# Soft MoE behind an attention, one core: w1's rows dealt to the partitions by chunks of 128, and the slot sums reading x in packed columns

## The chip, the core and the metric

The kernel runs on one core of one Trainium2 chip. The metric is the device time of one execution in microseconds (us); lower is better. TensorE (PE, with its weight loads as PEld), VectorE (DVE), ScalarE (ACT) and GpSimd (POOL) work side by side, each through its own queue in order; transfers between DRAM and SBUF run on 16 DMA engines. All loads of this kernel are issued from POOL's queue and convert float32 to bf16 on the way; the stores of the output are issued from SP's.

## The reference

An attention over 8 batches, 12 heads, 448 tokens and heads of 64, with one more term in the softmax's sum, feeds a soft mixture of 8 experts with 4 slots each:

```python
def _attn_ref(q, k, v):
    scale = 1.0 / np.sqrt(q.shape[-1])
    scores = scale * np.matmul(q, k.transpose(0, 1, 3, 2))
    m = np.max(scores, axis=-1, keepdims=True)
    e = np.exp(scores - m)
    attn = e / (np.sum(e, axis=-1, keepdims=True) + np.exp(-m) + 1e-09)
    return np.matmul(attn, v)

def _moe_ref(x, phi, w1, w2):            # x (3584, 768), phi (768, 32)
    logits = x @ phi
    d = np.exp(logits - logits.max(0, keepdims=True))
    d /= d.sum(0, keepdims=True) + 1e-09
    slot_input = (d.T @ x).reshape(E, S_per_e, D)
    for e in range(E):                   # w1[e] (768, 1024), w2[e] (1024, 768)
        h = np.maximum(slot_input[e] @ w1[e], 0.0)
        slot_out[e] = h @ w2[e]
    c = np.exp(logits - logits.max(1, keepdims=True))
    c /= c.sum(1, keepdims=True) + 1e-09
    return c @ slot_out.reshape(n_slots, D)
```

Between the two, x is the attention's output with the heads side by side: a row for each token, 768 columns.

## The kernel before

**Attention.** The 96 heads are taken in 48 pairs. A loop of 49 steps, each of two half-steps (about 5 us a step), runs several pairs at once in different phases: `T` transposes q and k on PE (L205), `A` computes scores and their row maxima on DVE (L227, L231, L240), `Bk` scores once more with the maxima subtracted by a second product (L302, L305) and the exponentials on ACT (L308), `AV` the products with v (L339), `N1` and `N2` the division on POOL (L351, L367 to L376; on DVE for the last four pairs), which write x, and `PX` x's transposes, one pair two steps later (L399, copied by ACT in L405). Six pairs are one batch of 448 tokens: x of a batch lies in `x[:, i, :]` with 128 tokens on the partitions, four blocks i, and 768 columns; two such buffers alternate.

**Slots, batch by batch.** `P(b)` returns the pieces of the mixture's first part for a batch, which the loop places in later half-steps: logits (`l_mm`, L434: x transposed, 24 blocks of 128x128 as weights, phi's 32 columns streamed), the running maximum and the exponentials `cd`, then `s_mm`, the slot sums d.T @ x. `s_mm` (L482 to L490) fills one PSUM tile `ps_s` with 7 parts of 32 slots: for each of the KC = 6 parts j of x's columns four matmuls, one for each block i of tokens, with a 128x128 piece of x as weights and 32 columns of `cd` streamed, and then four matmuls with a column of ones, for the sums of d. `s_add` adds `ps_s` to `acc` on DVE (L499, L501 for the first batch). For the batches 0 to 5 `s_mm` is placed in every sixth step, the second half (the matmuls start at 88, 119, 149, 180, 211 and 241 us), for batch 6 in the 47th step (259 us); for batch 7 it runs behind the loop (273 us), where `s_last` (L506) writes the sums to `siT`.

**Which column of x is where.** `siT[p, j, slot]` is the stationary operand of the experts' first layer (`hidden`, L673), which multiplies it with `w_sb["w1", e][p, j, :]` and sums over partitions p and parts j. So the column of x that part j of the slot sums puts on partition p has to be the row of w1 that lies on p as part j. In the kernel before both are 6p + j: `load_part` (L107, L108) reads w1 and w2 of an expert as `"(p j) f -> p j f"`, six (w1) or eight (w2) neighbouring rows to a partition, and `s_mm` takes for part j every sixth column of x. w2's rows are matched in the same way by `turn` (L680), which takes every eighth column of the hidden layer.

**Loads.** All go through POOL's queue in program order, among POOL's other work. At the end of a step come, where it is their turn: q and k some steps ahead of their use (L141, 336 KB each), v (L145, L146), and w1 in halves of three rows per partition (`load_half`, L114, L115; 768 KB as bf16): the first half of an expert in the steps 1, 4, 7, 10, 13, 16, 22 and 25, the second in the step after; w2 of three experts in the same way from step 28. The tile W has room for these 11 weights and nothing else reads or writes it before the loop ends. The other five w2 go into R, the tile that holds the attention's buffers, piece by piece as these are done with (`part_at` from step 38, and L647, L648, L662, L663). The last piece is three rows of expert 7 (L663), into the place of an x buffer that the last `s_mm` reads.

**After the loop.** `hidden` for experts 0 to 3 and 4 to 7, `turn`, `slots` (L687: the second layer, with w2 streamed; experts 4 to 7 by halves of the columns), a rearrangement of the slots' outputs (L725), and c @ slot_out in 28 tiles of 128 tokens (L743), scaled on ACT and DVE (L749, L751) and stored in seven transfers (L754).

Of the kernel before, what the change touches and what calls it, by code (L numbers as in the profile page):

```python
# [31 lines left out]
def kernel(  # L32
# [17 lines left out]
    KC = DD // 128  # L50
# [53 lines left out]

    def load_part(i, z0, z1):
        kind, e = halves[i]
        src = (moe_w1 if kind == "w1" else moe_w2)[e].rearrange("(p j) f -> p j f", p=128)  # L107
        gdma(out=w_sb[(kind, e)][:, z0:z1, :], in_=src[:, z0:z1, :])  # L108

    def load_half(i, z, t=None):  # L110

        if t is not None:
            w_view(i, t)
        n = (KC if halves[i][0] == "w1" else FK) // 2  # L114
        load_part(i, z * n, (z + 1) * n)  # L115
# [6 lines left out]
    with ExitStack() as at:  # L122
# [290 lines left out]
        def P(b):  # L413
            l, new = lb[b % 2], lb[(b + 1) % 2][:, 4, :]
            eng = nc.gpsimd if b < B - 2 else nc.vector
            x = xb[b % 2]
# [65 lines left out]
            def s_mm():  # L482
                ps = pa([128, KC + 1, NS], F32, "ps_s")
                for j in range(KC + 1):
                    for i in range(4):

                        w = x[:, i, :].rearrange("p (d j) -> p j d", j=KC)[:, j, :] if j < KC else \
                            ones[:, int(i == 3):int(i == 3) + 1].to_broadcast([128, 128])
                        nc.tensor.matmul(ps[:, j, :], w, v["cd"][:, 4 + i, :], start=(i == 0), stop=(i == 3))  # L489
                v["ps_s"] = ps  # L490
# [25 lines left out]
            if b < B - 1:  # L516
                return [both(lambda: l_mm(range(KC)), l_ev, c_max), both(l_turn, c_sub), both(s_max, d_sub),
                        both(exps, corr)] + ([c_turn, both(s_mm, s_add)] if late(b) else [both(s_mm, s_add), c_turn])
            return [lambda: l_mm(range(PB - 2)),
                    lambda: l_mm([PB - 2]),  # L520
                    both(lambda: l_mm([PB - 1]), l_ev, l_turn, lambda: keep_busy(2), s_max,
                         d_sub, lambda: exps(4, 8), corr, lambda: keep_busy(5), s_mm, s_last, lambda: keep_busy(2),
                         c_max, c_sub, lambda: exps(0, 4)),
                    c_turn]
# [50 lines left out]
        for s in range(NPAIR + 1):  # L575
# [69 lines left out]
            for i, z0, z1 in part_at.get(s, ()):  # L645
                load_part(i, z0, z1)
        load_part(14, 1, 8)  # L647
        load_part(15, 0, 1)  # L648
        nc.vector.reduce_max(fold, ident.rearrange("p (i s) -> p s i", i=4), axis=AX.X)
# [135 lines left out]
```

## Time and profile before

| | us |
|---|---|
| median of 3 runs (lowest to highest) | 321.62 (321.37 to 322.61) |
| the profiled execution, its own time | 321.49 |
| span of its profile | 319.7 |

| engine | busy us | share of the span | instructions |
|---|---|---|---|
| PE | 284.4 | 89% | 5072 |
| PE's weight loads (beside PE) | 165.9 | 52% | 5074 |
| DVE | 253.0 | 79% | 575 |
| ACT | 250.1 | 78% | 546 |
| POOL | 194.6 | 61% | 402 |
| DMA, the queue of POOL's loads | 31776 packets, 42.52 MB | 81.8% of 16 engines | 106 issues |

The mean granted clock of PE is 0.951 of full speed. In the chain of waits that ended last PE has 53% of the span, DVE 22% and ACT 11%; line 489 of the slot sums has 3%.

How to read it: the busy shares are means over a long loop and a tail that have different limits. In a timeline or chain row the first number is the start and the second the length in us, L489 is line 489 of the kernel, `ps_s<-cd,R` names the tile that is written and those that are read, and brackets give the idle time of that engine just before the row and what ended it. PEld is the load of a matmul's stationary operand; it runs beside the matmul before it. The length of one matmul holds its way through the array, so a row of matmuls that follow each other is read by the distance of their starts. A DMA row is the issue on its engine; the transfer lands later. In the table of windows the columns are: window, its length, then busy us and the number of instructions for PE, PEld, DVE, ACT and POOL, the granted clock, the share of the 16 DMA engines' time that packets took (over 1 where packets overlap) and the GB/s written.

### The profile page before, as it was taken

Reading aid. Unit: us, or ns where it says so; the run is one execution under the profiler, and the core shown is the slowest. Engines: PE = TensorE matmul, PEld = TensorE weight load, DVE = VectorE, ACT = ScalarE, POOL = GpSimd, SP = SyncE. Lnnn points to the kernel's source line nnn. Section 1 sums busy time; section 2 is a strip of 40 time slices with the busy share of each in tenths; the row PEclk is TensorE's granted clock in tenths of the full one; section 3 lists DMA queues with packets and bytes.
Section 4 is the critical chain, followed back from the end, with each engine's and each line's share of the span. In section 5 each row is a group of like instructions: output and inputs, shape, how many; then the busy total and the mean of one; then the engine's idle time right before and its main releaser. Section 6 shows DMA issues by size and latency. Waiting matters only on the chain.

```text
span 319.7 us, 12146 instructions
## 1 busy us (share of the span) xinstructions
PE 284.4 (89%) x5072; PEld 165.9 (52%) x5074; DVE 253.0 (79%) x575; ACT 250.1 (78%) x546; POOL 194.6 (61%) x402
## 2 busy tenths in 40 slices
PE   2898999999999999999999999999999997997800
PEld 1444556555566566656656665566555555561100
DVE  5888999998989989997999799989998354337910
ACT  2367699999989998999999999999998983217800
POOL 8651797868768968695978688867775723100000
PEclk9999999999999999999999999999999999897555
DMA  7990799999999999678999999997445899964998
GB/s 87 143 135 4 105 208 203 187 193 162 184 180 162 197 148 180 86 112 146 187 154 187 180 170 162 182 193 130 76 51 100 149 157 193 200 126 178 425 431 344
DMA packets 32838, 54.30 MB, mean 170 GB/s; under 512 B 2576, under 2 KB 27920, under 8 KB 32272
## 3 DMA queue, kind: packets, MB, share of 16 engines
q0 software_dynamic: 31776, 42.52, 81.8%
q1 hardware_dynamic: 1008, 11.01, 8.2%
q8 instruction: 39, 0.64, 0.7%
q14 instruction: 15, 0.12, 0.1%
HBM read 85.03 MB, written 11.01 MB: 300 GB/s over the span
## 4 chain that ended last, share of the span: by engine, by line
PE 53%; DVE 22%; ACT 11%; issue 4%; DMA 3%; POOL 2%; POOLq 0%; ACTq 0%
DVE mx L231 15%; PE ps_b L302 11%; PE ps_av L339 11%; PE ps_a L227 9%; PE ps_b L305 7%; PE ps_t L205 5%; ACT R L308 5%; DMA R<-in_moe_w_dram 3%; PE ps_s L489 3%; PE ps_o L743 3%; ACT R L208 2%; DVE mx L240 2%; DVE R L210 2%; ACT R L405 2%; ACT W L749 2%
## 5 line engine op out<-in xcount | busy, mean ns | idle before, releaser
L308 ACT ACTIVATE R<-ps_b 128x448 bf16<-128x448 f32 x336 | 158.3, 560 | 13.4 <-PE ps_b L305 9.9
L231 DVE TENSOR_REDUCE mx<-ps_a 128x1 f32<-128x448 f32 x288 | 160.7, 615 | 9.5 <-PE ps_a L227 9.0
L302 PE MATMUL ps_b<-R 64*128 64x448 bf16 (+1 forms) x384 | 82.6, 358 | 2.1 <-ACT R L405 1.8
L305 PE MATMUL ps_b<-mT,sel 64*128 64x448 bf16 (+1 forms) x384 | 78.9, 352 | 0.0
L227 PE MATMUL ps_a<-R 64*128 64x448 bf16 x288 | 68.8, 364 | 5.3 <-DVE mx L231 2.9
L367 POOL TENSOR_TENSOR R<-ubuf,rec 128x384 bf16<-128x384 f32 x44 | 36.3, 824 | 47.9 <-DVE rec L361 22.4
L339 PE MATMUL ps_av<-R 128*128 128x65 bf16 (+1 forms) x1536 | 64.8, 196 | 0.1
L339 PEld LDWEIGHTS <-R 128*128 128x128 bf16 (+1 forms) x1536 | 50.2, 100 | 23.9 <-issue 19.7
L205 PEld LDWEIGHTS <-R 64*64 64x64 bf16 x1344 | 31.1, 113 | 16.6 <-issue 6.1
L205 PE MATMUL ps_t<-ident,R 64*64 64x64 bf16 x1344 | 31.5, 197 | 5.3 <-DMA R<-in_q_dram 4.3
L302 PEld LDWEIGHTS <-R 64*128 64x128 bf16 (+1 forms) x384 | 19.4, 97 | 30.5 <-issue 25.6
L305 PEld LDWEIGHTS <-sel 64*128 64x128 bf16 (+1 forms) x384 | 21.3, 97 | 23.2 <-issue 15.9
L405 ACT CAST R<-ps_x 128x512 bf16<-128x512 f32 x47 | 27.9, 593 | 6.3 <-PE ps_x L399 6.2
L240 DVE TENSOR_REDUCE mx<-ps_a 128x1 f32<-128x448 f32 x48 | 29.6, 617 | 0.4 <-PE ps_a L237 0.3
L208 ACT COPY R<-ps_t 128x896 bf16<-128x896 bf16 x20 | 18.4, 918 | 10.8 <-PE ps_t L205 10.8
L351 ACT COPY ubuf<-ps_av 128x455 f32<-128x455 f32 x44 | 25.1, 571 | 1.2 <-PE ps_av L339 1.0
L227 PEld LDWEIGHTS <-R 64*128 64x128 bf16 x288 | 17.8, 94 | 14.5 <-issue 3.6
L376 POOL TENSOR_TENSOR R<-ubuf,rec 128x128 bf16<-128x128 f32 x44 | 17.6, 400 | 3.7
L237 PE MATMUL ps_a<-R 64*64 64x448 bf16 x96 | 18.5, 381 | 0.6 <-DVE mx L231 0.6
L399 PE MATMUL ps_x<-ident,R 128*128 128x128 bf16 x192 | 18.7, 218 | 0.0
L247 POOL TENSOR_SCALAR R<-mx 64x6 bf16<-64x6 f32 (+5 forms) x51 | 13.6, 266 | 8.1 <-DVE mx L231 4.7
L108 POOL DMA_DIRECT2D R<-in_moe_w_dram x15 | 8.4, 566 | 15.7 <-PE ps_s L489 6.7
(126 smaller groups left out, 368.5 us busy)
## 6 DMA issues: line engine op xcount, KB each, us to landing
W<-in_moe_w_dram POOLq DMA_DIRECT2D x22, 768.0 KB, 10.2
out_dram<-W SPq DMA_DIRECT2D x3, 2688.0 KB, 11.2
R<-in_v_dram POOLq DMA_DIRECT2D x32, 192.0 KB, 6.0
R<-in_q_dram POOLq DMA_DIRECT2D x15, 336.0 KB, 6.0
R<-in_k_dram POOLq DMA_DIRECT2D x15, 336.0 KB, 7.3
R<-in_moe_w_dram POOLq DMA_DIRECT2D x3, 768.0 KB, 7.7
out_dram<-W SPq DMA_DIRECT2D x3, 768.0 KB, 4.3
R<-in_moe_w_dram POOLq DMA_DIRECT2D x1, 1344.0 KB, 11.5
```

The source lines that it names most:

```text
L205: nc.tensor.transpose(ps[r, a, c:c + 64], src[r, pl, tok * D:(tok + 1) * D], ident[r, r])
L208: nc.scalar.copy(t, ps)
L227: nc.tensor.matmul(pss[hl][:, 0:S], t[r, 0, i * 128:(i + 1) * 128], t[r, 1, :], start=True, stop=True)
L231: nc.vector.reduce_max(mx[g][:, c:c + 1], pss[hl][:, 0:S], axis=AX.X)
L240: nc.vector.reduce_max(mx[g][:, c:c + 1], ps[:, 0:S], axis=AX.X)
L302: nc.tensor.matmul(outs[hl], t[rs[hl], 1, cols], t[rs[hl], 0, :], start=True, stop=False)
L305: nc.tensor.matmul(outs[hl], sel[rs[hl], 2 * pl + hl:2 * pl + hl + 1].to_broadcast([64, m]), mT[mg(n)][rs[hl], :], start=False, stop=True)
L308: nc.scalar.activation(e, p[:, 0:S], AF.Exp, scale=scale)
L339: nc.tensor.matmul(o, eT[n, i, hl][:, qc], vp[g % 2][:, 2 * pl + hl, i, 0:W65], start=(i == 0 and u == 0 and hl == 0), stop=(i == 3), skip ...
L351: (nc.scalar.copy if on_pool(n) else nc.vector.tensor_copy)(u, src)
L367: eng.tensor_mul(x[:, 0:3, c:c + 128].rearrange("p i (h d) -> p i h d", h=2), u[:, 0:6, 0:D].rearrange("p (i h) d -> p i h d", h=2), rec[: ...
L405: nc.scalar.copy(xT[:, pb, :], pss[0])
```

## The change

Two lines. w1's rows are dealt to the partitions by chunks of 128: part j on partition p is now row 128j + p. The slot sums take for part j the 128 neighbouring columns of x from 128j on, so that the same column of x meets the same row of w1. w2 is loaded as before.

```diff
     def load_part(i, z0, z1):
         kind, e = halves[i]
-        src = (moe_w1 if kind == "w1" else moe_w2)[e].rearrange("(p j) f -> p j f", p=128)
+        src = (moe_w1 if kind == "w1" else moe_w2)[e].rearrange("(j p) f -> p j f" if kind == "w1" else "(p j) f -> p j f", p=128)
         gdma(out=w_sb[(kind, e)][:, z0:z1, :], in_=src[:, z0:z1, :])
...
                 for j in range(KC + 1):
                     for i in range(4):
 
-                        w = x[:, i, :].rearrange("p (d j) -> p j d", j=KC)[:, j, :] if j < KC else \
+                        w = x[:, i, j * 128:(j + 1) * 128] if j < KC else \
                             ones[:, int(i == 3):int(i == 3) + 1].to_broadcast([128, 128])
                         nc.tensor.matmul(ps[:, j, :], w, v["cd"][:, 4 + i, :], start=(i == 0), stop=(i == 3))
```

The order of instructions is the same on every engine; on POOL the 16 loads of w1 change from 128 runs of 3072 elements to 128 x 3 runs of 1024.

## The prediction

> **What bounds the kernel now.** I read the page first: PE, DVE and ACT are each busy for 78 to 89% of the span, so no one engine explains it and the stage around the change has to be read by itself. Then the instructions of the two lines that do the same kind of product with a strided and an unstrided stationary operand (min/median/max ns):
>
> ```profile
> L489 PEld LDWEIGHTS <-R x192: 124/144/152, 88.1 to 274.7; 128*128 128x128 bf16 x192
> L489 PE MATMUL ps_s<-cd,R x192: 189/198/234, 88.2 to 274.7; 128*128 128x32 bf16 x192
> ...
> L434 PEld LDWEIGHTS <-R x192: 95/96/99, 64.8 to 270.8; 128*128 128x128 bf16 x192
> L434 PE MATMUL ps_l<-phi_sb,R x192: 176/176/190, 64.8 to 270.8; 128*128 128x32 bf16 x192
> ```
>
> Same shapes, 128x128 loaded and 128x32 streamed; the weights of L489 step 6 elements, those of L434 step 1. A duration is not a rate, so next the timeline (start us, length us, engine) around the first slot sum and around one block of L434:
>
> ```profile
> 88.13 1.20 PEld L489 LDWEIGHTS <-R 128*128 128x128 bf16 x24
> 88.16 1.27 PE L489 MATMUL ps_s<-cd,R 128*128 128x32 bf16 x24
> ...
> 89.27 0.25 PE L489 MATMUL ps_s<-cd,ones 128*128 128x32 bf16 x4
> 89.35 0.23 PEld L399 LDWEIGHTS <-R 128*128 128x128 bf16 x4
> 89.37 0.38 PE L399 MATMUL ps_x<-ident,R 128*128 128x128 bf16 x4
> 89.56 0.39 DVE L501 COPY acc<-ps_s 128x224 f32<-128x224 f32 x1 [1.33 <-PE ps_s L489]
> ...
> 89.79 0.59 ACT L405 CAST R<-ps_x 128x512 bf16<-128x512 f32 x1 [0.60 <-PE ps_x L399]
> ```
> ```profile
> 64.82 0.75 PE L434 MATMUL ps_l<-phi_sb,R 128*128 128x32 bf16 x24
> 65.51 0.32 PE L339 MATMUL ps_av<-R 128*64 128x65 bf16 x8
> ```
>
> From the first strided matmul to the first `ones` matmul, 88.16 to 89.27, 24 pairs take 1.11 us, 46.2 ns each. In L434 24 pairs take 65.51 - 64.82 = 0.69 us, 28.7 ns each. While the slot sum runs, DVE stands idle for 1.33 us behind it and ACT for 0.60 us behind the transposes queued after it (brackets): at this spot PE alone sets the pace. The same brackets stand at the sums near 119, 149, 181 and 212 us (1.40 and 0.60), and 0.94 and 0.94 near 242 us.
>
> The chain of waits (start, length) and the PE timeline then tell what sets the end:
>
> ```profile
> 275.17 11.12 DMA R<-in_moe_w_dram
> 286.30 0.04 issue
> 286.34 1.96 PE ps_so L687 x41
> ```
> ```profile
> 286.34 1.95 PE L687 MATMUL ps_so<-R,W 128*32 128x384 bf16 x41 [0.19 <-DMA R<-in_moe_w_dram]
> ```
>
> The last piece of w2 lands at 286.3 and PE waits only 0.19 us for it: two paths meet there, PE's and that of the transfers. Busy time by windows (the last two columns are the DMA share and GB/s written) and the POOL timeline say since when the transfers are backlogged:
>
> ```profile
> 256.00:260.00 4.00, 3.87 (x67) 2.28 (x62) 2.06 (x7) 4.00 (x11) 1.14 (x3) 1.00 0.82 122
> 260.00:264.00 4.00, 4.00 (x67) 2.17 (x66) 2.60 (x9) 3.12 (x8) 0.76 (x2) 1.00 1.11 202
> 276.00:280.00 4.00, 4.00 (x76) 2.05 (x69) 0.86 (x4) 1.99 (x4) 0.00 (x0) 1.00 1.03 199
> ```
> ```profile
> 255.48 1.66 POOL L108 DMA_DIRECT2D R<-in_moe_w_dram  x3 [1.00 <-PE ps_b L305]
> ```
>
> Three loads are issued at 255.48, released by PE; from about 258 on the queue is full at some 200 GB/s until 286. So a PE that is faster before 255 moves the end; what it gains after 255 meets a full queue.
>
> **The change, part by part.**
>
> *Slot sum without a stride* (L487/489). No instruction is added, removed or moved. Each of the 8 sums has 24 affected pairs. The new pitch is bounded below by the `ones` pairs of L489, whose weights step 0: 89.27 to 89.37, 4 pairs in 0.10 us, 25 ns; above by today's 46.2 ns (no gain). I take 28.7 ns from L434, which has the same shapes and a packed operand. Gain per sum: 24 x (46.2 - 28.7) = 0.42 us (0 to 0.51). It is less than the 0.60 us that ACT and the 1.33 us that DVE now wait there, so all three engines, and POOL, which waits for ACT's copy, start the next step 0.42 us earlier, and everything behind follows.
>
> Six sums (88, 119, 149, 180, 211, 241 us) lie before the issue at 255.48: 6 x 0.42 = 2.5 us. The seventh (259 us) and the eighth (273 us) advance PE by 0.84 us more, but the queue is full by then, so the last landing moves from 286.3 to about 283.8 only. PE's wait there grows from 0.19 to 0.19 + 0.84 = 1.0 us. What stands behind the landing (rest of L687, L725, output, stores) is unchanged and moves by 2.5 us.
>
> *w1 dealt by chunks* (L107). The 16 loads of half an expert's w1, issued between 36 and 165 us, have the same bytes; each partition's one run of 12 KB in DRAM (6 KB written) becomes three of 4 KB (2 KB written). w2's loads, which set the tail, keep theirs. Two costs:
>
> POOL's issue: L108 with 128 runs takes 0.57 us; L141 with 384 runs (3 per partition, the new count) 0.76 to 0.81. So +0.19 to +0.24 us, at most 3.8 us on POOL in all. It is covered by POOL's idle time: behind the issue at 103.31 comes L469, and then L367 after 0.41 us of idle; behind that at 87.41, 2.4 us of idle; the shortest I found is 0.32 us at 44 us. L367's product is transposed by PE two steps (about 10 us) later. Without this cover the cost would be its 3.8 us.
>
> The transfer: the queue is nearly full in this stage (the window 36 to 128 us has a DMA share of 1.09 and 183 GB/s, against 200 in the tail). The issues of 41 to 46 us and their times to landing:
>
> ```profile
> W<-in_moe_w_dram POOLq DMA_DIRECT2D x1, 768.0 KB, 10.7
> R<-in_q_dram POOLq DMA_DIRECT2D x1, 336.0 KB, 6.6
> R<-in_k_dram POOLq DMA_DIRECT2D x1, 336.0 KB, 7.5
> ```
>
> Issued at 41.57 (q), 42.40 (k) and 43.15 (w1), they land at 48.16, 49.86 and 53.86: k, in runs of 896 B, takes 1.70 us behind q, 202 GB/s; w1, in runs of 6 KB, 4.00 us, 197 GB/s. In a full queue short runs are as fast as long ones: 0. The other bound is from the trace's packet records (median ns by bytes written: 896 in 88, 3072 in 248, 6144 in 474): some 22 ns a packet plus 73.6 ns per KB of 1000 bytes. Three of 2048 B then take 3 x 173 = 519 for 474 ns; with 8 partitions on each of 16 DMA engines that is +0.36 us per load. I take 0 on the path, because the loads behind have slack: k issued at 102.55 lands at 109.5 and is first read at 117.8 (8.3 us); v issued at 94.92 lands at 100.6 and POOL copies it at 106.4 (5.8 us). Two loads per three steps, +0.72 us, do not use that up; w1 itself is read after 266 us.
>
> Sum: -2.5 us on 321.49, the profiled execution's own time (span 319.7 and 1.8 around it), gives 319.0. The median of the runs shown, 321.62, is 0.13 above that execution; I leave the forecast at 319.0.
>
> **Rivals.**
>
> *All eight sums count.* If the queue in the tail has some room after all (in the 4 us before 260 its share is 0.82), or the later issues also bring it forward, the end moves by 8 x 0.42 = 3.4 us, at most 8 x 0.51 = 4.1: 318.1, down to 317.4. Against it: the landings from 264.6 to 286.3 follow one another at 200 GB/s without a gap.
>
> *The stride costs nothing, no change.* If what makes L489 slow is not the step but where the tile lies or the order of its sums, the gain is 0: 321.5. Against: the transposes of L680, with a step of 8, also load in 146 to 148 ns at the median, those of L399, step 1, in 97. The Trainium skill ("SBUF — State Buffer", "Door 1: The DMA port swizzle") gives 8 elements as the step that bf16 may take for free in SBUF's lines of 16 bytes. By that figure a step of 6 is free and this would be the outcome; the trace disagrees with 144 against 96 ns. (The same place asks for two accesses to a line; 12 bytes apart they mostly don't share one, and by that condition the trace agrees.)
>
> *w1's new runs are slow in DRAM: slower.* One partition's three runs lie 512 KB apart, and no load of this trace reads so. Between two groups of three steps (about 15.6 us apart) the queue works 8.0 us on w1, 3.4 on q and k and 1.8 on v, so some 2.4 us are free. With x us more per w1 load, the backlog grows by 2x - 2.4 + 0.2 a group (0.2 being half of a sum's gain), over 6 groups, until v's 5.8 us are gone; then PE waits. It eats the 2.5 us gain at 6 (2x - 2.2) = 5.8 + 2.5, so x = 1.8, a load of 5.8 instead of 4.0 us. At x = 2.5 it would be 16.8 - 5.8 - 2.5 = 8.5 us slower: 330. Against it: even the first loads, with start-up, ran at 135 to 143 GB/s on the page's strip (5.6 us for such a load, x = 1.6).
>
> **How the numbers follow.** Forecast, six sums: 0.61. All eight: 0.18. No change: 0.10. Slow w1: 0.11. Below 0.5%, 1.6 us, a measurement of this kernel can't be told from no change. Faster takes the first two, 0.79; a little of the first could fall under 1.6 us, and a little of the third over it. Same 0.10, slower 0.11. The likeliest case alone spans 318.4 (pitch 25 ns) to 319.6. The range reaches down to all eight sums at their bound, 317.4, and up to just under no change, 321.3; it leaves out some 0.2.
>
> **What would show it.** Right: L489's weight loads near 96 ns; the 24 pairs in 0.69 us; ACT's wait before L405 in those steps about 0.18, DVE's before L499 about 0.98; sums 0.42 us earlier each time; L108's issues at 0.8 us; 4096 packets more; the last landing near 283.8, with PE waiting about 1 us for it in L687. Wrong: L489 still at 140 ns; w1 landing more than 13 us after its issue; a wait of L205 for q or k after 40 us; a last landing before 283 (all eight) or after 285.

## The result and the profile after

| | us, median (lowest to highest) | runs |
|---|---|---|
| before, beside the changed kernel | 321.69 (321.37 to 322.61) | 4 |
| changed | 318.13 (317.18 to 319.22) | 4 |
| ratio | 0.988, 95% interval 0.986 to 0.991 | |

The kernel is 1.2% faster; 319.0 had been forecast. Two more measurements, on other occasions, gave 0.991 (0.988 to 0.993) and 0.989 (0.985 to 0.992). The profiled execution of the changed kernel took 317.18 us with a span of 315.4 (before: 321.49 and 319.7).

First the instructions of the slot sums' line, by stationary operand (count, min/median/max ns), and who waits for them (us in all, times; 6.5 for this row before), after:

```profile
L489 PEld LDWEIGHTS <-R x192: 95/96/151, 87.6 to 270.8; 128*128 128x128 bf16 x192
L489 PE MATMUL ps_s<-cd,R x192: 176/176/234, 87.7 to 270.8; 128*128 128x32 bf16 x192
...
  DVE acc L499: 4.0, 5
```

The weight loads fell from 144 to 96 ns, the value of L434's. The rate shows in the timeline of the first sum:

```profile
86.90 0.77 POOL L108 DMA_DIRECT2D W<-in_moe_w_dram  x1
...
87.65 0.75 PE L489 MATMUL ps_s<-cd,R 128*128 128x32 bf16 x24
...
88.25 0.25 PE L489 MATMUL ps_s<-cd,ones 128*128 128x32 bf16 x4
...
88.36 0.38 PE L399 MATMUL ps_x<-ident,R 128*128 128x128 bf16 x4
88.54 0.39 DVE L501 COPY acc<-ps_s 128x224 f32<-128x224 f32 x1 [0.82 <-PE ps_s L489]
...
88.78 0.59 ACT L405 CAST R<-ps_x 128x512 bf16<-128x512 f32 x1
```

From the first matmul to the first one with `ones`, 87.65 to 88.25, 24 pairs take 0.60 us, 25.0 ns each, against 46.2 before: exactly the pitch of the `ones` pairs beside them. DVE's wait fell from 1.33 to 0.82 us (0.51 less). ACT's bracket of 0.60 us is gone; 0.60 less 0.51 leaves 0.09, and the views show no bracket that short. The first line is the issue of a half of w1 with its 384 runs, 0.77 us.

How far the kernel has come by each sum is read from the start of ACT's copy L405 behind it in the two traces. Measured from the value just ahead of each, the shift grows by one step a sum (minus is earlier):

```
us in the trace of before    68     90    120    151    182    212    243    261
shift of ACT's stream      -0.50  -1.02  -1.52  -2.04  -2.56  -3.06  -3.71  -4.24
```

Seven sums, 0.51 each (the sixth has 0.14 of another origin in it). The first 0.50 stands ahead of any sum; it is a gap of the other execution. In the trace of before, PE's timeline has this row; after, the same instruction (at 67.63) has no bracket, and in a second profile of the kernel before it has none either:

```profile
68.13 0.19 PE L268 MATMUL ps_m<-ident,R 128*128 128x64 bf16 x1 [0.39 <-issue]
```

Such gaps in which PE waits for nothing that the profile shows (near 68, 154 or 221 us, 0.2 to 0.6 us each) and a stretch near 20 us that cost 1.3 to 1.4 us came in some executions and not in others. Single spans can't be compared closer than that; medians and distances inside one trace can.

The end, in the chain of waits after:

```profile
279.03 0.64 PE ps_ht L680 x8
279.86 4.16 PE ps_so L687 x96
284.04 0.49 ACT W L721
```

and POOL's issues of the last w2 loads, whose brackets say what released them:

```profile
251.47 1.05 POOL L108 DMA_DIRECT2D R<-in_moe_w_dram  x2 [0.18 <-PE ps_b L305]
256.46 0.53 POOL L108 DMA_DIRECT2D R<-in_moe_w_dram  x1 [3.94 <-PE ps_s L489]
...
271.28 0.54 POOL L108 DMA_DIRECT2D R<-in_moe_w_dram  x1 [2.92 <-PE ps_s L489]
```

The last piece of w2, issued at 271.28, lands at 282.01, 4.29 us earlier than before (286.30). Before, the chain ran through that transfer for 11.12 us; now it stays on PE, whose 96 products of L687 run through without a wait. So this execution has the landing 1.8 us ahead of the forecast's 283.8 and none of the 1.0 us wait foreseen. The row to note is the load at 256.46: it waits for the seventh slot sum, which by the forecast could not matter.

The page's line on the queue of POOL's loads (packets, MB, share of 16 engines) and the groups of POOL's issues into W (count, busy us, mean ns):

```profile
q0 software_dynamic: 35872, 42.52, 83.9%
```
```profile
L108 POOL DMA_DIRECT2D W<-in_moe_w_dram x22 | 16.3, 742 | 0.2 <-issue 0.2
```

Exactly 4096 packets more (31776 before), the same bytes. The 22 issues into W take 16.3 us, 13.3 before: 3.0 us over the 16 halves of w1, 0.19 each.

### The profile page after: what moved, and what is told of

Same layout as the page of the kernel before. It is cut to its first block, busy times and chain, and to the rows that moved or that the text cites. A ratio compares the mean times of both kernels' runs of the same rounds, so it can differ in the third digit from the quotient of the medians.

```text
span 315.4 us, 12151 instructions
## 1 busy us (share of the span) xinstructions
PE 280.6 (89%) x5072; PEld 162.8 (52%) x5074; DVE 252.6 (80%) x575; ACT 249.8 (79%) x546; POOL 196.9 (62%) x402
## 3 DMA queue, kind: packets, MB, share of 16 engines
q0 software_dynamic: 35872, 42.52, 83.9%
## 4 chain that ended last, share of the span: by engine, by line
PE 54%; DVE 24%; ACT 12%; issue 3%; POOL 1%; ACTq 0%; POOLq 0%
DVE mx L231 16%; PE ps_b L302 10%; PE ps_av L339 10%; PE ps_a L227 9%; PE ps_b L305 7%; ACT R L308 6%; PE ps_t L205 5%; PE ps_o L743 2%; DVE mx L240 2%; DVE R L210 2%; ACT R L208 2%; PE ps_x L399 2%; PE ps_s L489 2%; ACT W L749 2%; PE ps_h L673 2%
## 5 line engine op out<-in xcount | busy, mean ns | idle before, releaser
L339 PE MATMUL ps_av<-R 128*128 128x65 bf16 (+1 forms) x1536 | 64.8, 196 | 0.1
L339 PEld LDWEIGHTS <-R 128*128 128x128 bf16 (+1 forms) x1536 | 50.1, 100 | 23.3 <-issue 19.1
L205 PEld LDWEIGHTS <-R 64*64 64x64 bf16 x1344 | 31.0, 113 | 16.5 <-issue 6.0
L205 PE MATMUL ps_t<-ident,R 64*64 64x64 bf16 x1344 | 31.4, 197 | 5.3 <-DMA R<-in_q_dram 4.1
L405 ACT CAST R<-ps_x 128x512 bf16<-128x512 f32 x47 | 27.9, 594 | 2.7 <-PE ps_x L399 2.2
## 6 DMA issues: line engine op xcount, KB each, us to landing
R<-in_moe_w_dram POOLq DMA_DIRECT2D x1, 1344.0 KB, 11.5
```

The lines of the kernel that those rows point to most:

```text
L205: nc.tensor.transpose(ps[r, a, c:c + 64], src[r, pl, tok * D:(tok + 1) * D], ident[r, r])
L339: nc.tensor.matmul(o, eT[n, i, hl][:, qc], vp[g % 2][:, 2 * pl + hl, i, 0:W65], start=(i == 0 and u == 0 and hl == 0), stop=(i == 3), skip ...
L405: nc.scalar.copy(xT[:, pb, :], pss[0])
```

## Experiments

The forecast rests on three claims: the gain is the slot sums' alone, dealing w1 costs nothing, and only the six sums ahead of the last stretch of transfers count.

### Each part alone

The slot sums alone: the edit at L487 of the change, with w1 loaded as before.

```diff
-                        w = x[:, i, :].rearrange("p (d j) -> p j d", j=KC)[:, j, :] if j < KC else \
+                        w = x[:, i, j * 128:(j + 1) * 128] if j < KC else \
```

> The slot sums read x in packed columns, w1 stays dealt as before; so the hidden layer multiplies columns of x with the wrong rows of w1, with the same shapes and transfers. My theory now: each of the eight sums gains 24 x (46.2 - 25.0) = 0.51 us and all eight reach the end, 4.1 us less than before, with 0.5 us of scatter either way. The theory of the prediction (only the six sums ahead of the tail count): 6 x 0.51 = 3.1 us less. A rival, that dealing w1 brings part of the gain (shorter packets let PE's instruction fetches through, 0.5 us at 68 us of the trace): here only 3.1 to 3.6 us less, and the idle gap of PE at 68 us still there.

Measured: 318.95 against 321.9, ratio 0.991 (0.988 to 0.994), 2.9 us less. By the interval at most 3.8 us are gained, so the 4.1 of all eight sums is out, and the 3.1 of six fits. The idle gap at 68 us is not in this profile.

Dealing w1 alone:

```diff
-        src = (moe_w1 if kind == "w1" else moe_w2)[e].rearrange("(p j) f -> p j f", p=128)
+        src = (moe_w1 if kind == "w1" else moe_w2)[e].rearrange("(j p) f -> p j f" if kind == "w1" else "(p j) f -> p j f", p=128)
```

> w1 is dealt by chunks, the slot sums still read every sixth column; so columns of x and rows of w1 don't match, with the same shapes. My theory: the transfers are covered, within 0.3 us of before. Rival 1, shorter packets help the instruction fetches: 0.5 us less or better, with no gap of PE at 68 us. Rival 2, the longer issue on POOL or the slower transfers cost: 0.4 us or more above before. In the trace L108 takes 0.77 instead of 0.57 us on POOL, and 4096 packets more.

Measured: 322.43, ratio 1.001 (0.998 to 1.003). The halves of w1 land 6.7 to 10.9 us after their issue (6.7 to 11.5 in the kernel before), and no product of L205 waits for q or k after the start. Nearly the whole gain comes from the sums; the rival of slow runs in DRAM, which needed 1.8 us more a load, is out. The interval still allows a cost of up to 1.1 us or a gain of up to 0.5, so a cost of 0.4, the second rival, is not excluded by this run alone. A gain of 0.5 through the gap at 68 us, the first, is at the other edge of it; the gap itself stands in four of the seven profiles of kernels with w1 as before and in none of the seven with w1 by chunks.

### Which sums count

```diff
-                        w = x[:, i, :].rearrange("p (d j) -> p j d", j=KC)[:, j, :] if j < KC else \
+                        w = (x[:, i, j * 128:(j + 1) * 128] if b < 6 else
+                             x[:, i, :].rearrange("p (d j) -> p j d", j=KC)[:, j, :]) if j < KC else \
```

The first six sums packed, w1 as before:

> Only the sums of batches 0 to 5 are packed, w1 as before; these six batches' slot inputs then don't match w1's rows. Theory that all sums count: 6 x 0.51 = 3.1 us less than before, and 1.0 us more than with all eight packed. Theory of the prediction, that the queue of transfers is full before the last two sums: the same time as with all eight packed, within 0.3 us.

Measured: 319.53, ratio 0.993 (0.990 to 0.996), 2.4 us less than 321.9. The pitch is 25 ns in the first six sums and 46.5 to 46.9 in the last two. This is 0.6 us slower than all sums packed (318.95, measured beside it), between the two theories (0.3 at most, and 1.0), and the intervals overlap: the run does not decide. And with `b >= 6`, the last two alone:

> Only the sums of batches 6 and 7 are packed, w1 as before; the slot inputs of these two don't match w1's rows. Theory that all sums count: 2 x 0.51 = 1.0 us less than before. Theory of the prediction: at most the 0.2 us that PE waits for the last load, so no change; PE's wait for the last piece of w2 grows from 0.19 to about 1.0 us.

Measured: 321.52, ratio 1.000 (0.998 to 1.002). Its timeline of PE (in this kernel L687 is line 688):

```profile
286.38 1.95 PE L688 MATMUL ps_so<-R,W 128*32 128x384 bf16 x41 [1.93 <-DMA R<-in_moe_w_dram]
```

PE waits 1.93 us for the last piece (0.19 before), which lands at 286.34 (286.30 before). By the two sums it would have been 0.19 + 1.02 = 1.21; the rest goes with a higher granted clock from 268 to 276 us, 1.00 instead of 0.88 and 0.69. All of it went into the wait; the interval of the ratio leaves room for up to 0.7 us of gain.

### The changed kernel again, and the kernel before

> The changed kernel once more, with more rounds. My theory: what counts is the slot sums alone, so the same as with packed sums and w1 dealt as before (0.9911 of before, 2.9 us less), within 0.5 us. Rival: dealing w1 adds to it, and the 0.9882 of the result (3.8 us less) comes back.

Measured: 318.73, ratio 0.991 (0.988 to 0.993). The shift of ACT's stream against the first trace is -0.28 ahead of the first sum and about 0.5 more for each: -0.80, -1.28, -1.81, -2.23, -2.75 behind the first five, and -3.7 at the last landing. The gain is 2.9 us of the 321.59 beside it, the value of the sums alone; the 3.8 of the rival did not come back.

> The kernel before, for a second profile: which of the small shifts between the traces are scatter of one execution. The gap of PE at 68 us (0.39 us, put down to issue) and the 1.0 us of POOL ahead of the three loads at 255.5 us come back if they belong to the program, and don't if they are scatter. Time as before, 321.9 within 1.5 us.

Measured, one execution: 322.66, span 320.9. PE's gap at 68 us is not in it. The wait of 1.00 us ahead of the three loads (255.48 in the first trace, 256.21 here) is.

### The price by step

Each batch's sums read x with another step, 1 to 6, and 2 and 3 once more:

```diff
-                        w = x[:, i, :].rearrange("p (d j) -> p j d", j=KC)[:, j, :] if j < KC else \
+                        z = (1, 2, 3, 4, 5, 6, 2, 3)[b]
+                        w = x[:, i, 0:128 * z].rearrange("p (d j) -> p j d", j=z)[:, j % z, :] if j < KC else \
```

> w1 dealt as before; the slot sums of batch 0 to 7 read x with a step of 1, 2, 3, 4, 5, 6, 2 and 3 elements, 128 of them from the first columns, so their values are others. Read are the starts of the 24 pairs in each sum. If SBUF serves steps of up to 8 bf16 for free (the Trainium skill's figure): 25 ns a pair at every step; the 46 ns at 6 already speaks against it. If two accesses to a line of 16 bytes are what it takes: 25 ns at steps 1 to 4, 46 ns at 5 and 6. If the cost goes with the bytes passed over: 25, 29, 33, 38, 42, 46 ns.

PE's timeline of this kernel (the line is 490 here), for the steps 2 to 6 in turn:

```profile
119.07 0.75 PE L490 MATMUL ps_s<-cd,R 128*128 128x32 bf16 x24
119.67 0.25 PE L490 MATMUL ps_s<-cd,ones 128*128 128x32 bf16 x4
...
149.22 0.79 PE L490 MATMUL ps_s<-cd,R 128*128 128x32 bf16 x24
149.86 0.25 PE L490 MATMUL ps_s<-cd,ones 128*128 128x32 bf16 x4
...
179.41 0.94 PE L490 MATMUL ps_s<-cd,R 128*128 128x32 bf16 x24
180.20 0.25 PE L490 MATMUL ps_s<-cd,ones 128*128 128x32 bf16 x4
...
209.75 1.10 PE L490 MATMUL ps_s<-cd,R 128*128 128x32 bf16 x24
210.70 0.25 PE L490 MATMUL ps_s<-cd,ones 128*128 128x32 bf16 x4
...
240.28 1.27 PE L490 MATMUL ps_s<-cd,R 128*128 128x32 bf16 x24
241.40 0.25 PE L490 MATMUL ps_s<-cd,ones 128*128 128x32 bf16 x4
```

The distance of the two starts by 24 is the pitch. From the unrounded starts, with step 1 and the repeats:

```
step           1     2     3     4     5     6  |   2     3
ns a pair   25.1  25.1  26.4  32.9  39.8  46.6  | 25.0  26.3
```

The step makes the price: 2 and 3 cost the same in another batch and buffer. At 1 and 2 nothing shows above 25 ns; from 3 on each further element of step adds 6.5 to 6.9 ns. None of the three theories fits as it stands. The third, bytes passed over, fits from 3 on if the pitch can't fall below 25 ns: a line through steps 4 and 6, 6.85 ns an element (an estimate from these figures), gives 26.1 at 3 and 19 at 2, below the 25. The rule of the Trainium skill weighed in the prediction ("SBUF — State Buffer", "Door 1: The DMA port swizzle"), by which bf16 strides up to 8 elements for free where a line of 16 bytes is hit twice, does not describe these loads: steps below 8 are not free, and step 4, where two elements share a line, already costs 7.8 ns a pair.

### Do more runs slow a full queue?

In the tail, where the transfers set the end, w2 too is dealt by chunks, so that each of its runs, of up to seven rows before, holds one row; L680 then turns packed columns.

```diff
-        src = (moe_w1 if kind == "w1" else moe_w2)[e].rearrange("(j p) f -> p j f" if kind == "w1" else "(p j) f -> p j f", p=128)
+        src = (moe_w1 if kind == "w1" else moe_w2)[e].rearrange("(j p) f -> p j f", p=128)
...
-                nc.tensor.transpose(ps[:, kt, :], h[g].rearrange("p (d k) -> p k d", k=FK)[:, kt, :], ident)
+                nc.tensor.transpose(ps[:, kt, :], h[g][:, kt * 128:(kt + 1) * 128], ident)
```

> As the changed kernel, and w2 is dealt by chunks of 128 too, with the hidden layer's transposes taking packed columns to match. w2's transfers write runs of 1.5 KB, also in the tail, where the queue is full from the seventh sum to the last landing. If a full queue goes by bytes (197 against 202 GB/s for runs of 6 KB and 896 B in the trace of before), the time is that of the changed kernel within 0.5 us. If it goes by packets (474 ns for 6144 B, 4 x 135 for 4 of 1536 B, 14% more), the 21 us from the first load of the full queue to the last landing become 24, and the time is 2 to 3 us above the changed kernel.

Measured: 319.26, ratio 0.992 (0.989 to 0.995), 0.5 us above the changed kernel beside it (318.73) with overlapping intervals; the 2 to 3 us of a queue that goes by packets are out. Its queue and three windows of its tail (PEclk, DMA share and GB/s last):

```profile
q0 software_dynamic: 41376, 42.52, 85.3%
```
```profile
268.00:272.00 4.00, 3.94 (x37) 1.86 (x36) 1.48 (x6) 0.69 (x3) 0.81 (x2) 0.61 1.15 205
272.00:276.00 4.00, 3.99 (x73) 1.84 (x72) 1.53 (x8) 1.57 (x3) 0.74 (x1) 1.00 1.16 209
276.00:280.00 4.00, 4.00 (x81) 2.36 (x74) 0.82 (x2) 1.37 (x2) 0.00 (x0) 1.00 1.16 211
```

5504 packets more, and the full queue still writes 205 to 211 GB/s (199 to 212 from 272 to 284 us before); the packets' share there grew from 1.01 to 1.03 to about 1.16. The last landing comes 15.98 us behind that of the load which waits for the seventh sum (16.42 before, 16.33 after). In this queue bytes count, not runs, down to runs of 1.5 KB.

### Is w1's dealing worth anything through the earlier issue?

In every kernel with w1 by chunks the first of the three loads ahead of the seventh sum (255.48 before) goes out without the 1.00 us for which POOL waits in the others. Two kernels side by side on one chip, the changed one and the one with the sums alone:

> The changed kernel once more, beside the next run on the same chip. Theory (all of the gain is the slot sums'; dealing w1 by chunks is worth nothing): 318.5, and the same as the kernel with the packed sums alone within 0.5. Rival (w1 dealt by chunks brings the three loads at 255 us forward by 1.05 us, and so the last landing and the end): about 0.8 faster than the packed sums alone, and the last landing some 1 us earlier than there.

> The packed slot sums alone, w1 as before (the hidden layer multiplies columns and rows that do not belong together). Theory: 318.5, within 0.5 of the changed kernel on the same chip. Rival: 319.2, some 0.8 slower than it, with the three loads at about 253 us issued 1.0 us after POOL could have had them.

Measured: 318.81, ratio 0.989 (0.985 to 0.992), and 318.46, ratio 0.989 (0.986 to 0.993). The early issue is there in the first and absent in the second, but the second is 0.35 us faster and its last landing the earlier one (282.65 against 284.25). So the medians show none of the rival's 0.8 us; with six runs each, spread over 317.0 to 319.7, a difference of that size can't be excluded. Why the wait is gone was not settled: in the traces these loads wait for the same semaphores in both kernels.

### Is the queue full ahead of the seventh sum?

In the changed kernel one sum is computed three times over, the seventh (`b == 6`) or the eighth (`b == 7`):

```diff
-                    for i in range(4):
+                    for i in 3 * [0, 1, 2, 3] if b == 6 else range(4):
```

> The changed kernel with the seventh slot sum computed three times over (the last one stands, the result is the same): 56 pairs more at 25 ns, 1.4 us on PE at about 257 us, which the next load of w2 waits for. Read is the distance from the issue of the last of the three loads ahead of it to the last landing, which is 30.0 to 30.2 in three runs of the changed kernel. The prediction's theory (the queue has been full since those three loads, so what PE does at the seventh sum cannot move the last landing): 30.1 again. Rival (the load that waits for the seventh sum starts the full stretch, so the seventh sum counts): 31.5. The time itself is 1.4 more by either, since PE then comes 1.4 later to its last products.

> The same with the eighth slot sum, at about 271 us, which the last load waits for. Both theories hold the queue full there, so the distance from the third load's issue to the last landing stays at 30.1, and PE, 1.4 later, finds its data there. If the last load's issue sets the landing by itself, it is 31.5.

Measured from the traces, us after the issue of the third of the three loads:

```
kernel                 load behind     load of seven rows    last
                       7th sum issued   issued    landed     landing
before                      4.14         10.76     22.25      29.71
after, three profiles       4.5          11.1   22.3 to 22.7  30.03 to 30.21
seventh three times         5.67         12.52     24.32      31.93
eighth three times          4.47         11.12     22.55      29.89
```

The eighth sum behaves as forecast: 1.4 us more on PE, the landing where it was, and 318.97 us, inside the changed kernel's own range. The expectation that the time itself would grow by 1.4 in either case was wrong for it: PE had that room. The seventh does not: in its one execution the landing moves by 1.8 us, and the time is 322.28. PE's timeline and two windows of that kernel:

```profile
285.76 3.33 PE L687 MATMUL ps_so<-R,W 128*32 128x384 bf16 x41 [2.00 <-DMA R<-in_moe_w_dram]
```
```profile
260.00:264.00 4.00, 3.88 (x69) 2.13 (x63) 2.13 (x7) 3.87 (x9) 1.05 (x2) 1.00 0.90 148
...
268.00:272.00 4.00, 3.49 (x39) 1.84 (x39) 1.74 (x7) 1.09 (x5) 0.56 (x1) 1.00 0.95 157
```

PE waits 2.0 us for the last piece, and twice the queue wrote less than the 200 GB/s of a full one: 148 at 260 to 264, ahead of the load that waits for the seventh sum (out 1.2 us late), and 157 at 268 to 272, ahead of the load of seven rows (out 1.4 us late). So in the changed kernel lateness at the seventh sum was paid in full, as far as one execution shows it. (The 41 products then took 3.33 instead of 1.95 us at a lower granted clock, 0.77 and 0.80 from 284 to 292 us; that is the other 1.4 us of this execution.) The 318.97 of the eighth had luck in it too: its PE ran at full clock from 264 to 272 us, where the three profiles of the changed kernel had 0.52 to 0.84.

The same place can be read in the other profiles: the rate of the queue from 2 to 4 us behind the first matmul of the seventh sum, where the load that it released starts to write, and the last landing, in us behind that matmul:

```
kernels                                             profiles   GB/s         last landing
w1 as before, seventh sum at step 6                    3       190 to 207   27.14 to 27.61
w1 as before, seventh sum packed (once at step 2)      4       191 to 203   26.10 to 27.07
w1 by chunks, seventh sum at step 6                    1        98          26.63
w1 by chunks, seventh sum packed                       4       135 to 152   26.44 to 26.76
w1 and w2 by chunks, seventh sum packed                1       101          26.49
w1 by chunks, seventh sum three times                  1        84          28.48
```

With w1 as before, the queue is full at this place, as the prediction read it. With w1 by chunks it is not: the three loads ahead go out 0.9 us earlier against PE, are done earlier, and the queue runs low until the seventh sum lets the next load go. So the change itself took the backlog away.

## Why the prediction was right, and where it was off

**The slot sums on the path: right.** PE alone sets the pace at these places. What the pairs save, ACT's stream gains, 0.51 us for each of the first seven sums.

**The pitch: mis-sized.** "I take 28.7 ns from L434, which has the same shapes and a packed operand" named the right row and read it wrongly. Its 0.69 us ran to the start of L339. In the trace of before the starts of those 24 matmuls lie 25 ns apart, 576 ns from the first to the last, and another 106 ns pass until L339, which streams 65 columns instead of 32: the 682 ns hold that gap. The `ones` pairs of L489, taken as the bound below, showed the pitch itself. Six sums are 6 x 0.51 = 3.1 us instead of 2.5: 318.4.

**Which sums count: the step that failed in part.** "The seventh (259 us) and the eighth (273 us) advance PE by 0.84 us more, but the queue is full by then." For the eighth this holds as to the last landing: computed three times, it left it where it was. For the seventh it does not hold in the changed kernel, where 1.4 us more on PE moved the landing by 1.8. The row that could have warned stands in the trace of before:

```profile
260.73 0.54 POOL L108 DMA_DIRECT2D R<-in_moe_w_dram  x1 [3.58 <-PE ps_s L489]
```

A full queue at this moment says nothing of the moment after the change: this load goes out when the seventh sum is done, and the loads ahead of it had come forward.

Whether the seventh's own 0.51 us reach the landing is another question, and stays open. In the table above the packed seventh sum has the landing earlier with w1 as before (26.7 against 27.4 us in the mean, the ranges not quite touching), and not with w1 by chunks (26.6 in either case, the strided one a single profile). The landing of the result, 4.29 us earlier than in the first trace of before, could be made up of 0.50 (the gap at 68 us), 7 x 0.51 and 0.14; but the second trace of before has its landing at 287.49, and w1's dealing alone brings it as close to the seventh sum. A last landing before 283, listed as a sign of all eight sums, came in two of the three profiles of the changed kernel (282.01, 282.60 and 284.25): it was no sign that single executions can give.

How much of the seventh's 0.51 the median holds is not settled. Five measurements of kernels with all sums packed lie 3.6, 2.9, 3.4, 3.0 and 3.7 us under the kernel before, 3.3 in the mean, between six sums (3.1) and seven (3.6). The first six alone gave 2.4, the last two alone 0.1 with an interval that reaches 0.7.

**PE's wait in L687: not in the profile of the result.** There PE ran at 0.52 and 0.63 of its clock from 264 to 272 us (before: 1.00, then 0.88 and 0.69 in the next 8 us), and its lead over the trace of before shrank from 4.24 us behind the seventh sum to 3.48 at the start of the eighth, more than the eighth sum gives. The second profile of the changed kernel has no wait either, at 0.61 and 0.54 of the clock; the third, at 0.84 and 0.73, has one:

```profile
284.29 1.95 PE L687 MATMUL ps_so<-R,W 128*32 128x384 bf16 x41 [0.64 <-DMA R<-in_moe_w_dram]
```

The two profiles of the kernel before have 0.19 and 0.48, so the 1.0 us of the forecast can't be checked here. Where there is no wait, PE's own work ends last, and there an eighth sum at the old pitch would have shown in the time: the forecast has no term for that.

**w1: right as to its cost.** The issues cost 0.19 us each, on POOL's idle time, and the loads land as soon as before; the time alone is 1.001, with a cost of up to 1.1 us inside the interval. The cover foreseen for loads that take longer was not needed. That it brings the three loads ahead of the seventh sum forward was not foreseen.

**The rivals.** No change through the stride: out, the step makes the price. Slow w1: out. All eight sums: no, with 4.1 us outside the interval of the sums alone and 3.3 in the mean; that its time of 318.1, from a pitch too long by 3.7 ns, meets the first measurement of 318.13 is luck. The forecast fell short by 0.9 us there and by 0.6 in the mean of the five: 0.6 is the pitch.

## What to carry to other kernels

Read the pitch of back-to-back weight loads from the distance of their starts, and from a row of the same line if there is one; a packed stationary operand (or a step of 2) is worth the re-dealing of whatever must match its order when PE sets the pace there. Re-dealing by longer lists of runs costs issue time, and nothing was seen to be lost in a queue that is already bound by bytes. Before you write off a gain because a queue is full, look at what releases the next load, and at whether the change moves the loads ahead of it: a backlog read in the trace of before may be gone after.

## What the runs showed of the hardware

- The price of a weight load with its matmul, by step (128x128, bf16, 32 columns streamed): 25.1 ns a pair at steps 1 and 2, 26.4 at 3, then 32.9, 39.8 and 46.6 at 4, 5 and 6.
- Splitting w1's runs from 6 KB into three of 2 KB written, and nothing else, left the rate from 36 to 128 us at 183 GB/s (183 before), though in the changed kernel the packets' own time over the span is 3.1 us of all 16 engines longer (83.9% of 315.4, 81.8% of 319.7 before). Splitting w2's into runs of 1.5 KB left the full queue of the tail at 205 to 211 GB/s.
- Executions differ by PE gaps of 0.2 to 0.6 us at the same few places and by where in the tail the lower granted clock falls (0.52 and 0.63 from 264 to 272 us in one, 0.77 and 0.80 from 284 to 292 in another). Behind the last landing it cost 1.4 us: 41 products took 3.33 instead of 1.95 us.
